# Gate products with the activations as stationary operand, woven between expert products

## The chip, the cores and the metric

The kernel runs on one core of one Trainium2 chip. The metric is the device time of one execution in microseconds. A core has a matrix engine (TensorE, PE in the profile; its loads of stationary operands are shown as PEld), a vector engine (DVE), an activation engine (ACT), GpSimd (POOL) and a queue engine (SP). Each engine takes its own instructions in order and waits for the others through semaphores.

## What is computed

Eight batches of grouped-query attention (16 query heads, 4 key and value heads, 384 positions, head size 64), then a mixture of experts over the 8 x 384 = 3072 tokens of 1024 values. A gate picks one of 4 groups and then one of 4 experts of that group for each token; the token goes through that expert's two layers alone, and its result is scaled by the gate's two probabilities.

```python
attn = softmax(scale * q @ k.T) @ v               # per batch and head
x = attn.transpose(0, 2, 1, 3).reshape(3072, 1024)
g_logits = x @ w_group                            # 1024 x 4
g_idx = argmax(g_logits, axis=1)
e_logits = xg @ w_expert[g]                       # 1024 x 4, for the tokens of group g
e_idx = argmax(e_logits, axis=1)
h = relu(xg[mask_e] @ w1[g, e])                   # 1024 x 1024
out[tok_idx] = g_w * e_w * (h @ w2[g, e])         # 1024 x 1024
```

Both gates together are 20 columns (`NW`): 4 for the groups, 16 for the experts.

## The kernel before

**Stages.** The order of the instructions is written out by hand. For each batch b from 2 on there is an attention stage (`Attn.run`) and then a block (`block(b)`). The block runs the experts' layers for batch b - 1 on PE, while DVE and ACT normalise the attention output of batch b and cast it to bf16. Batches 0 and 1 are arranged apart: batch 0's first expert layer stands inside the attention of batch 1, and `first_block` holds its second layer.

**Attention.** A unit is one head group and one slice of 64 keys: four bf16 products for the scores (L305), the exponential on ACT (L311), then four f32 products with v (L324). There are 24 units in a batch. POOL adds pairs of exponentials (L331), DVE reduces them for the row sums (L338). Each group's output goes from PSUM to `xT[b]` (f32, 128 partitions x 8 x 384: the 1024 values of a token on partitions and 8 slices, tokens along the free axis). `xT[b]` of batch 1 lives in one of the two buffers of the expert weight w1.

**Normalisation.** `collect` sums what was reduced (L397), `sums` brings it to the right partitions with PE (L405), DVE takes the reciprocal (L409) and `normalise` spreads it and multiplies `xT` in place (L416, L425), a pair of slices at a time. `cast` makes bf16 (`xb`) of it on ACT (L432).

**The experts.** `moe_h` (L606) has 16 products of 384 columns per call, and four calls make the first layer; ACT applies the relu (L608). `ffn_y` (L615) makes the second layer for one chunk of 128 tokens: two halves of 8 products with 512 columns. `y_out` scales and stores.

**One expert per batch, by a guess.** The kernel guesses one expert for a whole batch ahead of time, fetches its weights, and runs all tokens of the batch through it, with zero weight for tokens that belong elsewhere. Whatever (batch, expert) pairs are left over are done in a loop at the end. The guess takes the mean of v over the positions: `guess_mean`, 12 products of 128x128 bf16 stationary operands with one column (L457), a copy to `vm`, and `guess_logits`, 4 products with 20 columns (L473). `first_choice` turns logits of batch 0's guess into a choice; for the other batches the guess is a further row of the gate's softmax. `pick_index` turns the choice into an index, and `pick`, `pick_w1` and `pick_w2` fetch weights on POOL's queue.

**The gate.** `gate_logits` holds the gate's weights stationary (32 columns for each of 8 slices, side by side in four column strips of the array) and lets the 384 tokens of `xT` stream past: 8 f32 products (L443). ACT copies the 32 x 4 partial rows to `lgs` (L447). `gate_tokens` then takes `lgs` as stationary operand, in three chunks of 128 tokens, against a 0/1 matrix that adds the four strips: the logits come out with tokens on partitions (L468, 3 f32 products). `gate_softmax` does the choice on DVE, and the closure it returns (`weights[b]`) later does the probabilities. In a block, `gate_logits` stands between the two halves of y of chunk 1, `gate_tokens` and `guess_mean` after that chunk, and `guess_logits` after the first half of chunk 2. Batch 1's gate stands inside the attention of batch 2, after units 3, 19 and 21 (`second_logits`, `second_gate`, `second_pick`).

PSUM is held in two pairs of tiles, named s and o; each new tile takes the other one of its pair, and waits until that one's last reader is done.

Of the kernel before, what the change touches and what calls it, by code (L numbers as in the profile page):

```python
# [18 lines left out]
def kernel(  # L19
# [51 lines left out]
    def ps_tile(which, shape=None, dtype=F32):  # L71
        if which == "x":
            which = f"o{1 - turn['o']}"
        else:
            turn[which] = 1 - turn[which]
            which += str(turn[which])
        return psum.tile(shape or [P, 2, 512], dtype, name="ps_" + which)
# [113 lines left out]
    cw_all = cpool.tile([P, B, SC, NE], F32)  # L191
    oh_all = cpool.tile([P, B, SC + 1, NE], BF16)
    nc.vector.memset(oh_all[:, B - 1, SC, :], 0.0)
    oh_first = cpool.tile([P, NE], BF16)
    oh1_all = cpool.tile([P, B, NE], F32)
    rem_f = cpool.tile([P, B, NE], F32)
# [41 lines left out]
    def evac(eng, out_, in_):  # L238
        if eng is nc.scalar:
            eng.copy(out=out_, in_=in_)  # L240
        else:
            eng.tensor_copy(out=out_, in_=in_)  # L242
# [190 lines left out]

    lgs = {}

    def gate_logits(b, pt):
        lg = pt[:, 0]
        for jj in range(KQ // 4):  # L440
            for t in range(4):
                kq = 4 * jj + t
                nc.tensor.matmul(out=lg[32 * t:32 * t + 32, :S], lhsT=wg[:, kq, :],  # L443
                                 rhs=xT[b][:, kq, :],
                                 start=(jj == 0), stop=(jj == KQ // 4 - 1))
        ls = gpool.tile([P, S], F32, name="lgs")
        nc.scalar.copy(out=ls, in_=lg[:, :S])  # L447
        lgs[b] = ls

    def guess_mean(b, pt, eng=None):  # L450

        pm = pt[:, 1, :Hkv]
        v16 = vraw[b].rearrange("p h x -> p (h x)").bitcast(BF16)
        for g in range(Hkv):
            for i in range(SC):
                e0 = g * NC * D + i * P
                nc.tensor.matmul(out=pm[:, g:g + 1], lhsT=v16[:, 2 * e0 + 1:2 * (e0 + P):2],  # L457
                                 rhs=onesb[:, :1], start=(i == 0), stop=(i == SC - 1))
        vm = gpool.tile([P, Hkv], BF16, name="vm")
        evac(eng or nc.vector, vm, pm)  # L460
        return vm

    def gate_rows(pt):
        return pt[:, 1, 64:64 + (SC + 1) * NW].rearrange("p (c n) -> p c n", n=NW)

    def gate_tokens(b, glp):
        for c in range(SC):
            nc.tensor.matmul(out=glp[:, c, :], lhsT=lgs[b][:, c * P:(c + 1) * P],  # L468
                             rhs=mod32[:, 0, :NW], start=True, stop=True)

    def guess_logits(vm, glp):
        for g in range(Hkv):
            nc.tensor.matmul(out=glp[:, SC, :], lhsT=vm[:, g:g + 1].to_broadcast([P, P]),  # L473
                             rhs=wgd[:, g, :], start=(g == 0), stop=(g == Hkv - 1))

    def gate_softmax(b, glp, guess, eng=None):

# [77 lines left out]
    e_is = {}  # L555

    def pick_index(b):
        oh = oh_first if b == 0 else oh_all[:, b - 1, SC, :]
        key = gpool.tile([P, NE], F32, name="key")
        nc.vector.scalar_tensor_tensor(key, oh, float(NE), eback, op0=ALU.mult, op1=ALU.add)  # L560
        km = gpool.tile([P, 1], F32, name="km")
        nc.vector.tensor_reduce(out=km, in_=key, axis=AX.X, op=ALU.max)
        oh1 = oh1_all[:, b, :]
        nc.vector.tensor_scalar(oh1, key, km, None, op0=ALU.is_ge)
        t1 = gpool.tile([P, NE], F32, name="t1")
        ef = gpool.tile([P, 1], F32, name="ef")
        nc.vector.scalar_tensor_tensor(t1, eidx, 1.0, oh1, op0=ALU.mult, op1=ALU.mult,
                                       accum_out=ef)
        e_i = gpool.tile([P, 1], I32, name="e_i")
        nc.vector.tensor_copy(out=e_i, in_=ef)  # L570
        e_is[b] = e_i
# [27 lines left out]
            j = 2 * c + h  # L599
            yield slice(h * H2, (h + 1) * H2), 2 * (j % SC) + j // SC  # L600

    def ffn_h(x, w1, hT, f0, which):
        h = ps_tile(which)
        for jj in range(2):
            for kq in range(KQ):
                nc.tensor.matmul(out=h[:, jj, :S], lhsT=w1[:, kq, (f0 + jj) * P:(f0 + jj + 1) * P],  # L606
                                 rhs=x[:, kq, :], start=(kq == 0), stop=(kq == KQ - 1))
        nc.scalar.activation(hT[:, f0:f0 + 2, :], h[:, :, :S], ACT.Relu)  # L608

    def ffn_y(w2, hT, c, which, nhs=(0, 1), y=None):  # L610
        if y is None:
            y = ps_tile(which)
        for nh in nhs:
            for f in range(FQ):
                nc.tensor.matmul(out=y[:, nh, :], lhsT=hT[:, f, c * P:(c + 1) * P],  # L615
                                 rhs=w2[:, f, nh * HALF:(nh + 1) * HALF],
                                 start=(f == 0), stop=(f == FQ - 1))
        return y

    hTs = {}  # L620

    def moe_h(b, f0, which):
        if f0 == 0:
            hTs[b] = xpool.tile([P, FQ, S], BF16, name="hT", bufs=1)
        ffn_h(xb[b], w1s[b], hTs[b], f0, which)

    def y_out(b, c, y, split=False):
        ot = opool.tile([P, DM], F32, name="ot")
# [6 lines left out]
        for ps, x in halves(c):  # L635
            nc.sync.dma_start(out=out_rows(out[b * S:(b + 1) * S])[x], in_=ot[ps])

    def moe_y(b, c, which):
        y_out(b, c, ffn_y(w2s[b], hTs[b], c, which))

    def do(f, *a):
        return lambda: f(*a)
# [21 lines left out]

    def first_guess():
        state["pt"] = ps_tile("x")
        state["vm"] = guess_mean(0, state["pt"], nc.scalar)

    def first_pick():
        glp = gate_rows(state["pt"])  # L670
        guess_logits(state["vm"], glp)
        first_choice(glp)
        pick_index(0)

# [46 lines left out]
        11: [do(cast, 0, 2)],  # L721
        13: [do(cast, 0, 3)],
    })
    moe_h(0, 0, "s")
    pt = ps_tile("x")
    gate_logits(0, pt)
    moe_h(0, 2, "s")
    glp = gate_rows(pt)
    gate_tokens(0, glp)
    vm = guess_mean(1, pt, nc.scalar)  # L730
    collect(1, 0, 2)
    sums(1, 0, 2, "s")
    for m in range(2):
        normalise(1, m)
    moe_h(0, 4, "s")
    guess_logits(vm, glp)
    weights[0] = gate_softmax(0, glp, True, nc.scalar)
    pick_index(1)
    moe_h(0, 6, "s")
# [3 lines left out]
    def first_block():  # L743

        prefetch(1)
        collect(1, 2, Hkv)
        weights[0]()
        out_weights(0)
        cast(1, 0)
        cast(1, 1)  # L750
        moe_y(0, 0, "s")
        y = ffn_y(w2s[0], hTs[0], 1, "s", (0,))
        sums(1, 2, Hkv, "o")
        normalise(1, 2)
        normalise(1, 3)
        ffn_y(w2s[0], hTs[0], 1, "s", (1,), y)
        y_out(0, 1, y)
        cast(1, 2)
        cast(1, 3)
        nc.sync.dma_start(out=xb_dram[1], in_=xb[1])  # L760
        y = ffn_y(w2s[0], hTs[0], 2, "o", (0,))
        at[2] = Attn(2)
        at[2].score(0)
        ffn_y(w2s[0], hTs[0], 2, "o", (1,), y)
        at[2].score(1)
        return {1: [do(y_out, 0, 2, y, True)], 3: [second_logits], 19: [second_gate],
                21: [second_pick]}

    def second_logits():
        gate_logits(1, ps_tile("x"))  # L770

    def second_gate():
        state["pt"] = ps_tile("x")
        gate_tokens(1, gate_rows(state["pt"]))
        state["vm"] = guess_mean(2, state["pt"])

    def second_pick():
        glp = gate_rows(state["pt"])
        guess_logits(state["vm"], glp)
        weights[1] = gate_softmax(1, glp, True, nc.scalar)  # L780
        pick_index(2)

    def prefetch(b):
        pick(b)
# [7 lines left out]
    def block(b):  # L792
        last = b == B - 1
        f = b - 1
        prefetch(b)
        moe_h(f, 0, "s")
        collect(b, 0, Hkv)
        weights[f]()
        out_weights(f)
        moe_h(f, 2, "s")  # L800
        sums(b, 0, Hkv, "o")
        for m in range(4):
            normalise(b, m)
        moe_h(f, 4, "s")
        moe_h(f, 6, "s")
        cast(b, 0)
        cast(b, 1)
        moe_y(f, 0, "s")
        cast(b, 2)
        cast(b, 3)  # L810
        nc.sync.dma_start(out=xb_dram[b], in_=xb[b])
        y = ffn_y(w2s[f], hTs[f], 1, "s", (0,))
        gate_logits(b, ps_tile("o"))
        ffn_y(w2s[f], hTs[f], 1, "s", (1,), y)
        y_out(f, 1, y)
        pt = ps_tile("s")
        glp = gate_rows(pt)
        gate_tokens(b, glp)
        vm = None if last else guess_mean(b + 1, pt)
        y = ffn_y(w2s[f], hTs[f], 2, "o", (0,))  # L820
        if not last:
            guess_logits(vm, glp)
            at[b + 1] = Attn(b + 1)
            at[b + 1].score(0)
        weights[b] = gate_softmax(b, glp, not last)
        if not last:
            pick_index(b + 1)
        ffn_y(w2s[f], hTs[f], 2, "o", (1,), y)
        if not last:
            at[b + 1].score(1)  # L830
            return {1: [do(y_out, f, 2, y, True)]}
        y_out(f, 2, y, True)
        weights[b]()
        out_weights(b)
# [120 lines left out]
```

The softmax here doesn't subtract the row's maximum and nothing guards it: scores larger than these inputs give would overflow.

## Time and profile before

| | us |
|---|---|
| median of 3 runs (381.98 to 382.19) | 381.99 |
| profiled execution | 381.92 |
| its span in the profile | 380.1 |
| PE busy | 364.6 |
| DVE busy | 261.9 |
| ACT busy | 232.6 |
| POOL busy | 147.3 |
| L468, 48 records with 20 columns | 6.0 |
| L443, 128 records with 384 columns | 12.0 |
| L447, 8 copies on ACT | 3.8 |

The span runs from the first to the last instruction that the profiler recorded; 1.8 us of the profiled execution lie around it. An f32 product appears as two weight loads and two matmul records. A matmul's recorded length has the array's latency in it, so the pace is read from the distance between starts. The granted clock of TensorE was 0.996 of full speed on average. One block and the attention before it repeat every 44.2 us.

### The profile page before, as it was taken

What the parts mean: (1) busy time and instruction counts of PE and PEld (TensorE: products, weight loads), DVE (VectorE), ACT (ScalarE), POOL (GpSimd) and SP (SyncE); (2) the same over time, 40 slices, a digit from 0 to 9 for tenths busy, and PEclk for the clock granted to TensorE, in tenths of its full rate; (3) what the DMA queues carried; (4) which work ended last, traced back from release to release, by engine and by line L of the source; (5) the groups of instructions that cost most, each with busy time, mean ns of one, the idle gap of its engine ahead of it and who ended that gap; (6) DMA issues with size and microseconds to landing.
All of it is one profiled execution on the core that took longest, in us unless ns stands there. A gap on an engine that the chain in (4) does not pass through costs nothing.

```text
span 380.1 us, 8950 instructions
## 1 busy us (share of the span) xinstructions
PE 364.6 (96%) x3663; PEld 193.9 (51%) x3663; DVE 261.9 (69%) x494; ACT 232.6 (61%) x315; POOL 147.3 (39%) x116
## 2 busy tenths in 40 slices
PE   8999799999989999999999999999999999999992
PEld 3444356444545455545555455554555456554541
DVE  4789978847689279854998279883798449983130
ACT  4779945768824498256953489344982569544321
POOL 5657730716613077212653047330772036600000
PEclk9999999999999999999999999999999999999998
DMA  8975999999999999899999999999998999199734
GB/s 190 247 115 93 238 211 149 241 237 260 207 160 223 252 248 184 173 211 297 213 148 221 228 278 208 148 220 254 244 185 163 182 282 228 30 207 220 236 68 100
DMA packets 71209, 76.02 MB, mean 200 GB/s; under 512 B 35928, under 2 KB 50264, under 8 KB 71168
## 3 DMA queue, kind: packets, MB, share of 16 engines
q0 software_dynamic: 26640, 41.03, 61.8%
q1 hardware_dynamic: 44096, 33.81, 36.1%
q10 hardware_dynamic: 432, 0.61, 0.5%
q8 instruction: 29, 0.48, 0.5%
q14 instruction: 12, 0.10, 0.1%
HBM read 89.21 MB, written 18.87 MB: 284 GB/s over the span
## 4 chain that ended last, share of the span: by engine, by line
PE 78%; DVE 13%; ACT 6%; issue 2%; ACTq 0%; DVEq 0%; POOLq 0%
PE ps_o L324 22%; PE ps_s L606 18%; PE ps_s L615 14%; PE ps_o L615 7%; PE ps_s L305 7%; ACT e L311 4%; DVE red L338 4%; PE ps_o L443 3%; DVE xT L425 2%; DVE rb L416 2%; PE ps_o L268 1%; PE ps_o L606 1%; DVE w L425 1%; PE ps_s L468 1%; PE ps_o L405 1%
## 5 line engine op out<-in xcount | busy, mean ns | idle before, releaser
L331 POOL TENSOR_TENSOR e<-e 128x768 f32<-128x768 f32 x64 | 116.1, 1830 | 138.5 <-ACT e L311 91.5
L311 ACT ACTIVATE e<-ps_s 128x768 f32<-128x768 f32 x192 | 149.1, 819 | 25.2 <-PE ps_s L305 23.5
L324 PE MATMUL ps_o<-e,v_raw 64*64 64x384 f32 x1536 | 153.8, 482 | 1.6 <-DVE xT L425 1.6
L338 DVE TRANSPOSE_TENSOR_REDUCE red<-e 128x24 f32<-128x768 f32 x128 | 114.1, 946 | 10.5 <-POOL e L331 10.5
L606 PE MATMUL ps_s<-xb,w 128*128 128x384 bf16 x480 | 81.0, 326 | 0.0
L324 PEld LDWEIGHTS ps_o<-e,v_raw 64*64 64x64 f32 x1536 | 61.0, 133 | 28.5 <-issue 20.0
L305 PE MATMUL ps_s<-qT,kT 64*64 64x384 bf16 x768 | 67.1, 327 | 3.0 <-ACT e L311 1.7
L608 ACT ACTIVATE hT<-ps_s 128x768 bf16<-128x768 f32 x30 | 24.3, 811 | 70.9 <-PE ps_s L606 70.9
L606 PEld LDWEIGHTS <-w 128*128 128x128 bf16 x512 | 48.8, 98 | 36.3 <-issue 4.8
L615 PEld LDWEIGHTS <-hT 128*128 128x128 bf16 x384 | 36.0, 98 | 45.4 <-issue 5.4
L615 PE MATMUL ps_s<-w,hT 128*128 128x512 bf16 x248 | 56.4, 379 | 0.0
L305 PEld LDWEIGHTS <-kT 64*64 64x64 bf16 x768 | 29.4, 104 | 42.6 <-issue 39.1
L615 PE MATMUL ps_o<-w,hT 128*128 128x512 bf16 x136 | 32.0, 379 | 0.0
L416 DVE STREAM_TRANSPOSE rb<-inv 128x384 f32<-128x384 f32 x60 | 31.1, 557 | 1.0
L425 DVE TENSOR_TENSOR xT<-xT,rb 128x768 f32<-128x768 f32 x26 | 28.2, 1086 | 0.9
L634 ACT ACTIVATE ot<-ps_s,we 128x1024 f32<-128x1024 f32 x14 | 15.6, 1116 | 19.1 <-PE ps_s L615 19.1
L432 ACT CAST xb<-xT 128x768 bf16<-128x768 f32 x28 | 22.1, 832 | 0.0
L371 DVE COPY xT<-ps_o 128x768 f32<-128x768 f32 x22 | 20.2, 919 | 0.0
L242 DVE CAST vm<-ps_s 128x4 bf16<-128x4 f32 x5 | 0.8, 163 | 27.4 <-PE ps_s L457 27.4
L663 POOL COPY after<-qT 128x1 bf16<-128x1 bf16 x7 | 1.3, 189 | 40.5 <-DMA qT<-q_raw 37.5
L631 DVE TENSOR_SCALAR ot<-ps_o,we 128x512 f32<-128x512 f32 x7 | 5.3, 750 | 15.6 <-ACT ot L630 11.3
L409 DVE RECIPROCAL inv<-ps_o 128x96 f32<-128x96 f32 (+2 forms) x10 | 6.0, 603 | 7.0 <-PE ps_o L405 7.0
(129 smaller groups left out, 189.3 us busy)
## 6 DMA issues: line engine op xcount, KB each, us to landing
w<-in_moe_w_dram POOLq DMA_DIRECT2D x16, 2048.0 KB, 21.9
out_dram<-ot SPq DMA_DIRECT2D x42, 256.0 KB, 7.0
xb_scratch<-xb SPq DMA_DIRECT2D x8, 768.0 KB, 9.8
q_raw<-in_q_dram POOLq DMA_DIRECT2D x7, 768.0 KB, 33.6
v_raw<-in_v_dram SPq DMA_DIRECT2D x14, 384.0 KB, 7.3
out_dram<-ot SPq DMA_DIRECT2D x11, 128.0 KB, 2.3
k<-in_k_dram POOLq DMA_DIRECT2D x7, 192.0 KB, 30.3
w<-in_q_dram POOLq DMA_DIRECT2D x3, 192.0 KB, 7.3
```

The source lines that it names most:

```text
L305: nc.tensor.matmul(out=sT[r * H2:(r + 1) * H2, s, :S], lhsT=kT[b][s * D:(s + 1) * D, slot, ks], rhs=qT[b][s * D:(s + 1) * D, kq * SC:(kq + ...
L311: nc.scalar.activation(e.rearrange("p t (s x) -> p s t x", s=2), sT[:, :, :S].rearrange("p s (t x) -> p s t x", t=2), ACT.Exp, scale=scale)
L324: nc.tensor.matmul(out=oT[t * D:(t + 1) * D, r, :S], lhsT=vraw[b][r * H2:(r + 1) * H2, g, c * D:(c + 1) * D], rhs=self.e[u][r * H2:(r + 1) ...
L331: eng.tensor_add(out=self.e[u], in0=self.e[u], in1=self.e[u + 1])
L338: nc.vector.tensor_reduce(out=reds[self.b][:, g, n].rearrange("p t j -> p (t j)"), in_=self.e[u].rearrange("p t (j x) -> p (t j) x", x=32) ...
L371: nc.vector.tensor_copy(out=dst, in_=src)
L416: nc.vector.transpose(out=rb[:, r].rearrange("p (j x) -> p j x", x=32), in_=inv[b][:, 2 * m + r].unsqueeze(2).to_broadcast([P, NB, 32]))
L425: eng.tensor_mul(out=x, in0=x, in1=rb)
L432: nc.scalar.copy(out=xb[b][:, ks, :], in_=xT[b][:, ks, :])
L606: nc.tensor.matmul(out=h[:, jj, :S], lhsT=w1[:, kq, (f0 + jj) * P:(f0 + jj + 1) * P], rhs=x[:, kq, :], start=(kq == 0), stop=(kq == KQ - 1))
L608: nc.scalar.activation(hT[:, f0:f0 + 2, :], h[:, :, :S], ACT.Relu)
L615: nc.tensor.matmul(out=y[:, nh, :], lhsT=hT[:, f, c * P:(c + 1) * P], rhs=w2[:, f, nh * HALF:(nh + 1) * HALF], start=(f == 0), stop=(f == ...
```

## The change

The gate is done in one step, with `xT` as stationary operand: for each chunk of 128 tokens, 8 f32 products of a 128x128 slice of `xT` with 20 columns of the gate's weights, added up in PSUM; 24 products in place of 8 + 3. `gate_logits`, the copy to `lgs` and the 0/1 matrix's product are gone. `gate_tokens`, `guess_mean` and `guess_logits` no longer emit their products but return them as a list, and `weave` emits such a list one by one, spread evenly behind the products of `ffn_h` or `ffn_y`.

In a block, the guess's means go into the fourth `moe_h`, and the gate and the guess logits into y of chunk 1. For batch 0 the means for batch 1 go into the first `moe_h` and the gate and guess logits into the second. The guess for batch 2 moves into `first_block`, as a choice of its own (`first_choice`), and batch 1's gate moves into the first two `moe_h` of block 2, where the normalisation of batch 2 is also put in another order.

```diff
+    def weave(main, side):
+        k = 0
+        for i, f in enumerate(main):
+            f()
+            while k < len(side) and k * len(main) < (i + 1) * len(side):
+                side[k]()
+                k += 1
+
+    def mm(*a, **kw):
+        return lambda: nc.tensor.matmul(*a, **kw)
+
+    def gate_tokens(b, glp):
+        return [mm(out=glp[:, c, :], lhsT=xT[b][:, kq, c * P:(c + 1) * P], rhs=wg[:, kq, :NW],
+                   start=(kq == 0), stop=(kq == KQ - 1))
+                for c in range(SC) for kq in range(KQ)]
...
-    moe_h(0, 0, "s")
     pt = ps_tile("x")
-    gate_logits(0, pt)
-    moe_h(0, 2, "s")
     glp = gate_rows(pt)
-    gate_tokens(0, glp)
-    vm = guess_mean(1, pt, nc.scalar)
+    moe_h(0, 0, "s", guess_mean(1, pt))
+    vm = mean_copy(pt, nc.scalar)
+    moe_h(0, 2, "s", gate_tokens(0, glp) + guess_logits(vm, glp))
     collect(1, 0, 2)
     sums(1, 0, 2, "s")
...
     moe_h(0, 4, "s")
-    guess_logits(vm, glp)
     weights[0] = gate_softmax(0, glp, True, nc.scalar)
     pick_index(1)
...
-        moe_y(0, 0, "s")
-        y = ffn_y(w2s[0], hTs[0], 1, "s", (0,))
+        pt = ps_tile("o")
+        glp = gate_rows(pt)
+        moe_y(0, 0, "s", guess_mean(2, pt))
+        vm = mean_copy(pt, nc.vector)
+        y = ffn_y(w2s[0], hTs[0], 1, "s", (0,), side=guess_logits(vm, glp))
+        first_choice(glp)
         sums(1, 2, Hkv, "o")
...
-        return {1: [do(y_out, 0, 2, y, True)], 3: [second_logits], 19: [second_gate],
-                21: [second_pick]}
+        pick_index(2)
+        return {1: [do(y_out, 0, 2, y, True)]}
...
-        moe_h(f, 0, "s")
+        gates = []
+        if f == 1:
+            glp = gate_rows(ps_tile("o"))
+            gates = gate_tokens(1, glp)
+        moe_h(f, 0, "s", gates[:12])
         collect(b, 0, Hkv)
-        weights[f]()
-        out_weights(f)
-        moe_h(f, 2, "s")
-        sums(b, 0, Hkv, "o")
-        for m in range(4):
-            normalise(b, m)
-        moe_h(f, 4, "s")
-        moe_h(f, 6, "s")
+        if f == 1:
+            sums(b, 0, Hkv, "o")
+            normalise(b, 0)
+            moe_h(f, 2, "s", gates[12:])
+            normalise(b, 1)
+            weights[f] = gate_softmax(f, glp, False)
+            normalise(b, 2)
+            moe_h(f, 4, "s")
+            normalise(b, 3)
+        else:
+            weights[f]()
+            out_weights(f)
+            moe_h(f, 2, "s")
+            sums(b, 0, Hkv, "o")
+            for m in range(4):
+                normalise(b, m)
+            moe_h(f, 4, "s")
+        pt = ps_tile("o")
+        glp = gate_rows(pt)
+        moe_h(f, 6, "s", [] if last else guess_mean(b + 1, pt))
+        if f == 1:
+            weights[f]()
+            out_weights(f)
         cast(b, 0)
         cast(b, 1)
+        guess = [] if last else guess_logits(mean_copy(pt, nc.scalar), glp)
         moe_y(f, 0, "s")
...
-        y = ffn_y(w2s[f], hTs[f], 1, "s", (0,))
-        gate_logits(b, ps_tile("o"))
-        ffn_y(w2s[f], hTs[f], 1, "s", (1,), y)
+        y = ffn_y(w2s[f], hTs[f], 1, "s", side=gate_tokens(b, glp) + guess)
         y_out(f, 1, y)
-        pt = ps_tile("s")
-        glp = gate_rows(pt)
-        gate_tokens(b, glp)
-        vm = None if last else guess_mean(b + 1, pt)
         y = ffn_y(w2s[f], hTs[f], 2, "o", (0,))
         if not last:
-            guess_logits(vm, glp)
             at[b + 1] = Attn(b + 1)
             at[b + 1].score(0)
```

More of the change, by code (lines that the diff above doesn't have):

```diff
@@ L193 @@
     nc.vector.memset(oh_all[:, B - 1, SC, :], 0.0)
+    nc.vector.memset(oh_all[:, 1, SC, :], 0.0)
     oh_first = cpool.tile([P, NE], BF16)
@@ L432, in cast, with guess_mean @@
         nc.scalar.copy(out=xb[b][:, ks, :], in_=xT[b][:, ks, :])
[L436 to L450, printed above, removed]
+    def weave(main, side):
[11 more added lines that the diff above has]
+                for c in range(SC) for kq in range(KQ)]
+    def guess_mean(b, pt):
         pm = pt[:, 1, :Hkv]
         v16 = vraw[b].rearrange("p h x -> p (h x)").bitcast(BF16)
+        side = []
         for g in range(Hkv):
@@ L456, in guess_mean, with mean_copy @@
                 e0 = g * NC * D + i * P
-                nc.tensor.matmul(out=pm[:, g:g + 1], lhsT=v16[:, 2 * e0 + 1:2 * (e0 + P):2],
-                                 rhs=onesb[:, :1], start=(i == 0), stop=(i == SC - 1))
+                side.append(mm(out=pm[:, g:g + 1], lhsT=v16[:, 2 * e0 + 1:2 * (e0 + P):2],
+                               rhs=onesb[:, :1], start=(i == 0), stop=(i == SC - 1)))
+        return side
+    def mean_copy(pt, eng):
         vm = gpool.tile([P, Hkv], BF16, name="vm")
-        evac(eng or nc.vector, vm, pm)
+        evac(eng, vm, pt[:, 1, :Hkv])
         return vm
@@ L464, in gate_rows @@
         return pt[:, 1, 64:64 + (SC + 1) * NW].rearrange("p (c n) -> p c n", n=NW)
[L466 to L469, printed above, removed]
     def guess_logits(vm, glp):
-        for g in range(Hkv):
-            nc.tensor.matmul(out=glp[:, SC, :], lhsT=vm[:, g:g + 1].to_broadcast([P, P]),
-                             rhs=wgd[:, g, :], start=(g == 0), stop=(g == Hkv - 1))
+        return [mm(out=glp[:, SC, :], lhsT=vm[:, g:g + 1].to_broadcast([P, P]), rhs=wgd[:, g, :],
+                   start=(g == 0), stop=(g == Hkv - 1)) for g in range(Hkv)]
     def gate_softmax(b, glp, guess, eng=None):
@@ L557, in pick_index @@
     def pick_index(b):
-        oh = oh_first if b == 0 else oh_all[:, b - 1, SC, :]
+        oh = oh_first if b in (0, 2) else oh_all[:, b - 1, SC, :]
         key = gpool.tile([P, NE], F32, name="key")
@@ L600, in halves, with ffn_h, ffn_y, moe_h @@
             yield slice(h * H2, (h + 1) * H2), 2 * (j % SC) + j // SC
-    def ffn_h(x, w1, hT, f0, which):
+    def ffn_h(x, w1, hT, f0, which, side=()):
         h = ps_tile(which)
[L604 to L607, printed above, removed]
+        weave([mm(out=h[:, jj, :S], lhsT=w1[:, kq, (f0 + jj) * P:(f0 + jj + 1) * P],
+                  rhs=x[:, kq, :], start=(kq == 0), stop=(kq == KQ - 1))
+               for jj in range(2) for kq in range(KQ)], side)
         nc.scalar.activation(hT[:, f0:f0 + 2, :], h[:, :, :S], ACT.Relu)
-    def ffn_y(w2, hT, c, which, nhs=(0, 1), y=None):
+    def ffn_y(w2, hT, c, which, nhs=(0, 1), y=None, side=()):
         if y is None:
             y = ps_tile(which)
[L613 to L617, printed above, removed]
+        weave([mm(out=y[:, nh, :], lhsT=hT[:, f, c * P:(c + 1) * P],
+                  rhs=w2[:, f, nh * HALF:(nh + 1) * HALF], start=(f == 0), stop=(f == FQ - 1))
+               for nh in nhs for f in range(FQ)], side)
         return y
     hTs = {}
-    def moe_h(b, f0, which):
+    def moe_h(b, f0, which, side=()):
         if f0 == 0:
             hTs[b] = xpool.tile([P, FQ, S], BF16, name="hT", bufs=1)
-        ffn_h(xb[b], w1s[b], hTs[b], f0, which)
+        ffn_h(xb[b], w1s[b], hTs[b], f0, which, side)
     def y_out(b, c, y, split=False):
@@ L636, in y_out, with moe_y @@
             nc.sync.dma_start(out=out_rows(out[b * S:(b + 1) * S])[x], in_=ot[ps])
-    def moe_y(b, c, which):
-        y_out(b, c, ffn_y(w2s[b], hTs[b], c, which))
+    def moe_y(b, c, which, side=()):
+        y_out(b, c, ffn_y(w2s[b], hTs[b], c, which, side=side))
     def do(f, *a):
@@ L666, in first_guess @@
         state["pt"] = ps_tile("x")
-        state["vm"] = guess_mean(0, state["pt"], nc.scalar)
+        for f in guess_mean(0, state["pt"]):
+            f()
+        state["vm"] = mean_copy(state["pt"], nc.scalar)
     def first_pick():
         glp = gate_rows(state["pt"])
-        guess_logits(state["vm"], glp)
+        for f in guess_logits(state["vm"], glp):
+            f()
         first_choice(glp)
@@ L765, in first_block @@
         at[2].score(1)
-        return {1: [do(y_out, 0, 2, y, True)], 3: [second_logits], 19: [second_gate],
-                21: [second_pick]}
[L769 to L780, printed above, removed]
         pick_index(2)
+        return {1: [do(y_out, 0, 2, y, True)]}
     def prefetch(b):
```

## The prediction

> **What bounds the kernel now.** I read the page first, engines and then the chain that ended last, then the busy time by stage, then the chain and PE's instructions in order of time inside one steady block. From the page, parts 1 and 4:
>
> ```profile
> PE 364.6 (96%) x3663; PEld 193.9 (51%) x3663; DVE 261.9 (69%) x494; ACT 232.6 (61%) x315; POOL 147.3 (39%) x116
> ...
> PE 78%; DVE 13%; ACT 6%; issue 2%; ACTq 0%; DVEq 0%; POOLq 0%
> ```
>
> PE is the bound, and the chain is PE for 78%. By stage (columns: stretch, its length, then busy us and instructions of PE, weight loads, DVE, ACT, POOL; then clock, DMA share, GB/s):
>
> ```profile
> 86.00:113.50 27.50, 25.39 (x315) 13.85 (x312) 20.34 (x40) 18.13 (x27) 12.50 (x7) 1.00 1.09 207
> ...
> 196.20:222.20 26.00, 25.83 (x190) 13.53 (x190) 16.42 (x41) 11.10 (x15) 4.13 (x7) 1.00 1.01 222
> ```
>
> The block of batch 4 (second line) has PE busy 25.83 of 26.0 us, so nothing absorbs work added there. The attention of batch 2 (first line) has 2.1 us of PE idle. The chain in block 4 (start, length, what):
>
> ```profile
> 207.22 5.18 PE ps_s L615 x24
> 212.40 1.43 PE ps_o L443 x16
> 213.83 1.83 PE ps_s L615 x8
> 215.66 0.58 PE ps_s L468 x6
> 216.24 0.28 PE ps_s L457 x12
> 216.53 1.75 PE ps_o L615 x8
> ```
>
> Gate and guess products stand bare on the path. Their prices come from the timeline of the weight loads and of PE there (start, length, engine):
>
> ```profile
> 215.29 0.85 PEld L468 LDWEIGHTS ps_s<-mod,lgs 128*128 128x128 f32 x6
> 215.98 0.46 PEld L457 LDWEIGHTS <-v_raw 128*128 128x128 bf16 x12
> ```
>
> ```profile
> 212.03 0.38 PE L615 MATMUL ps_s<-w,hT 128*128 128x512 bf16 x1
> 212.33 1.50 PE L443 MATMUL ps_o<-xT,wg 128*32 128x384 f32 x16
> 213.76 1.90 PE L615 MATMUL ps_s<-w,hT 128*128 128x512 bf16 x8
> 215.50 0.74 PE L468 MATMUL ps_s<-mod,lgs 128*128 128x20 f32 x6
> 216.09 0.44 PE L457 MATMUL ps_s<-onesb,v_raw 128*128 128x1 bf16 x12
> 216.39 1.89 PE L615 MATMUL ps_o<-w,hT 128*128 128x512 bf16 x8
> ```
>
> L468 has three f32 products of a 128x128 stationary operand with 20 columns in flight: six records, so an f32 product is two loads and two matmuls. The first load starts at 215.29, with the last expert product, and its matmul starts at 215.50, when that product has streamed (0.214 us): hidden. From 215.50 to 216.09, 0.59 us, there are five exposed f32 loads and the step to a bf16 one. In the single records the f32 loads start 0.111 us apart and the step is 0.029. The twelve bf16 loads of L457 go at 0.025 each (0.30 to 216.39).
>
> **What the Trainium skill says.** "TensorE: Matmul & The Clock Gate", section "LDWEIGHTS (loading the stationary operand)": a load takes its columns divided by 1.2 in ns, 107 for 128 columns; the trace has 111. The same page, "Weight-path perf modes — Fast Weight Load (FWL) and DoubleRow": 128-column loads that are not FP32 are fast; the trace has 25 ns against 111. The same page, "Step-by-step: what each phase is for": the next load is pulled ahead under the running matmul, into a background buffer; the trace shows one load ahead, never two. These three decide the forecast.
>
> **The change part by part.**
>
> *A gate product on its own between expert products.* Its first load hides (0.111 under 0.214, or under the 0.163 of a 384-column product: 16 take 2.65 with start). Then the second f32 load is exposed, 0.111, and then the next expert product's load, which was hidden before, 0.029: 0.140 in all. Two side by side: only the first of four loads hides, 3 x 0.111 + 0.029 = 0.363. No row shows such an alternation, so I bound it. If the expert load too were prefetched, a single costs 0.111. If no load hid, it costs 2 x 0.111 + 0.029 = 0.251. I take 0.140, since both switches of type are in the trace around L468.
>
> *Removed, per batch:* L443 from 212.24 (212.03 + 0.214) to 213.76, 1.52, with the array's change of shape at both ends; L468, 0.59; together 2.11. ACT's copy of lgs (0.48) goes too; ACT is busy 11.1 of 26 us there, so that is worth nothing.
>
> *Added, batches 2 to 6:* 28 side products (24 gate, 4 guess) among 16 main ones: the weave puts them 2, 2, 2, 1 after successive ones. The 24 gates fall as 10 pairs and 4 singles: 3.63 + 0.56 = 4.19. Net +2.08 each, **+10.4 for five**. Batch 7 has no guess: 8 pairs and 8 singles, 4.02, net **+1.91**. Batch 0 has the same 28 in 16: net **+2.08**; PE runs without a gap from 49.9 to 63.3, and DVE's normalisation and ACT wait behind its sums, so it lands on the path.
>
> *Guess products.* Twelve bf16 loads cost 0.30 bare. Woven, the guess's load hides but the expert's is exposed at the same 0.025, so 0.30 again: zero. The four guess logits likewise. The copy of vm moves from DVE to ACT (0.18), behind two casts and 3 us before it is needed: covered; without cover, 0.2 a block.
>
> *Batch 1, moved.* Attention 2 loses three pauses of PE: L443 behind DVE's ot (86.04 to 87.70, 1.66), L468 and L457 behind DVE's copy of xT (101.24 to 103.01, 1.77), L473 (104.65 to 104.94, 0.29): **-3.72**. DVE loses the 3.5 us of softmax and pick from 105.3, so the sums no longer wait at 111.8 (**-1.32**). They now stand one expert step earlier, 4.3 us after attention; DVE's rsum came 3.45 us after it in block 3, so they should find it ready. The gate in block 2: 12 + 12 in 16 + 16, all singles, 24 x 0.140 = **+3.36**. DVE's softmax there ends before guess_mean needs the bank of its logits, by some 2 us.
>
> *What the guess in block 1 makes late.* first_choice stands on DVE before the reciprocal of the sums. Its seven small operations took 1.50 us for batch 0 (27.04 to 28.54). The last guess logit ends near 76.5, so the reciprocal moves from 76.58 to 78.05; behind it stand two normalisations, ACT's last cast (which waited for DVE until 81.21), the first exp, and PE's third score at 82.80. That is **+1.47**, and it covers the 0.4 of guess products in front of it. pick_index(2) comes after them on DVE: covered.
>
> *Queues.* POOL's fetch of w1 for batch 2 now needs the gate's readers of xT[1], which lives in that buffer: done near 113.2, while POOL waits for a transpose until 114.75 anyway. If later, a weight needed at 154 that lands 22 us after its issue still has slack. SP's order is kept.
>
> *Sum:* 10.4 + 1.91 + 2.08 - 3.72 - 1.32 + 3.36 + 1.47 = **+14.2**. Span 380.1 + 14.2 = 394.3. The profiled execution took 381.92, 1.8 around the span, so 396.1; the median of the runs is 0.07 above it: **396**.
>
> **Rivals.**
>
> *Deep prefetch (ends faster).* If several loads could be waiting, the weight port alone would bound a woven stretch. With 512-column products: 48 x 0.111 + 16 x 0.025 = 5.73 against 3.43 of streaming, so gates cost 2.30, +0.19 over before, six times +1.1. Batch 0: 5.73 - 2.60 = 3.13, +1.0. Batch 1 over 32 products: 6.13 - 5.20 = 0.93 in place of 3.36, so its part is -2.64. Sum -0.5; without first_choice's 1.47, which ACT's slack could take, -2.0: **380.0**. It decides from the point where the second f32 load also hides. Against it: L468's loads keep step with its matmuls, one ahead.
>
> *Nothing hides.* 48 x 0.111 + 24 x 0.029 = 6.0 per batch: 7 x 1.8 + 2.7 more, **411**. It needs a drain at each switch of f32 and bf16; against it, the switch at 215.50 cost nothing and the one at 216.09 cost 0.029.
>
> *Absorbed in part.* Attention 2 falls to 19.9 us and the blocks give back a few waits; or pairs cost nearer 0.3: 24 x 6 products at 0.02 to 0.03 less is 3 to 4 us: **391**. Against it: block 4 has 0.17 us idle.
>
> *Within 0.2%.* Only if batch 1's gains were three times what I count. About 0.2% is what a measurement of this kernel can tell from no change.
>
> **How the numbers follow.** Forecast 0.80 (393 to 399), absorbed 0.10 (388 to 393), nothing hides or a new stall 0.06 (399 to 411), deep prefetch 0.03, unchanged 0.01. All but the last two are slower: 0.96. The range 391 to 400.5 leaves out the far part of the absorbed case and of the costly one.
>
> **What would show it.** In each block from batch 2 on: 48 gate records on PE where there were 22, and the 16 expert products of y's token chunk 1, which take 3.43 us bare, stretched to near 7.7. The period of a block goes from 44.2 to 46.3. Attention 2 runs without a gate, with its first exp 1.5 us late, and the sums after it don't wait. f32 loads of the gate under expert products, each second one exposed. Wrong if the woven stretch stays near 5.7, if an alternation costs other than 0.14 for a single and 0.36 for a pair, or if a wait for PSUM, DVE or a weight shows on PE where I saw none.

## The result

The changed kernel takes 400.49 us (median of 4 executions, 397.82 to 403.54) against 382.09 (381.98 to 382.35): a ratio of 1.0483, 95% interval 1.0384 to 1.0582. Its executions fall into two groups, two at 397.8 to 398.0 and two at 403.0 to 403.5; the profiled one, 402.96 with a span of 401.3, is of the second. The runs below show that this difference is the kernel's own. Of 34 executions of the kernel before that were taken with the later runs, one took 476.83 us at a mean clock of 0.754; it is left aside, and nothing here explains it.

From the page of the kernel after, parts 1, 2 (the granted TensorE clock in 40 equal slices, in tenths of full speed) and 4:

```profile
PE 385.7 (96%) x3871; PEld 232.6 (58%) x3871; DVE 262.1 (65%) x498; ACT 229.0 (57%) x311; POOL 147.2 (37%) x116
...
PEclk9999975999999999999999999999999999999998
...
PE 83%; DVE 8%; ACT 6%; issue 2%; ACTq 0%; DVEq 0%
```

PE is busy 21 us more, and its share of the chain goes from 78% to 83%. The clock line shows something that the profile of the kernel before does not have: two slices, from 50 to 70 us, with 0.7 and 0.5.

**A steady block.** Part of the block of batch 4 in order of time, PE and then the weight loads (start, length, engine; L447 is now the line of every product that goes through `mm`, so expert products are told from gate products by their shapes):

```profile
224.23 0.52 PE L447 MATMUL ps_o<-wg,xT 128*128 128x20 f32 x4
224.59 0.38 PE L447 MATMUL ps_s<-w,hT 128*128 128x512 bf16 x1
224.81 0.52 PE L447 MATMUL ps_o<-wg,xT 128*128 128x20 f32 x4
225.17 0.38 PE L447 MATMUL ps_s<-w,hT 128*128 128x512 bf16 x1
225.38 0.52 PE L447 MATMUL ps_o<-wg,xT 128*128 128x20 f32 x4
225.74 0.38 PE L447 MATMUL ps_s<-w,hT 128*128 128x512 bf16 x1
225.96 0.29 PE L447 MATMUL ps_o<-wg,xT 128*128 128x20 f32 x2
226.10 0.38 PE L447 MATMUL ps_s<-w,hT 128*128 128x512 bf16 x1
```

```profile
224.59 0.63 PEld L447 LDWEIGHTS ps_o<-wg,xT 128*128 128x128 f32 x4
225.06 0.18 PEld L447 LDWEIGHTS <-hT 128*128 128x128 bf16 x1
```

A pair stands between 224.81 and 225.17, 0.36 us; a single between 225.96 and 226.10, 0.14. These are the 0.363 and 0.140 of the prediction. The first load of a pair starts at 224.59 with the expert product and hides; the expert product's own load starts at 225.06, only after the pair's last load. A block and its attention repeat every 46.24 us in place of 44.2: +2.05, where +2.08 was predicted. The first expert products of two blocks on the chain (start, length, what):

```profile
209.44 5.31 PE ps_s L447 x32
255.68 5.31 PE ps_s L447 x32
```

**Batch 0's layer.** Busy time from its first expert product to the next score (stretch, length, busy us and instructions of PE, weight loads, DVE, ACT, POOL; then clock, DMA share, GB/s), then the waits of PE there. First the kernel before, then the profiled execution of the kernel after, then another execution of the same kernel, `a_again`, without the fall of the clock:

```profile
49.86:63.30 13.44, 13.44 (x114) 7.94 (x110) 9.87 (x18) 4.16 (x8) 2.22 (x2) 1.00 1.21 194
```

```profile
49.74:72.90 23.16, 22.05 (x140) 16.59 (x137) 10.69 (x21) 3.57 (x7) 2.23 (x2) 0.71 1.00 190
```

```profile
50.02:67.16 17.14, 15.81 (x140) 11.93 (x136) 10.30 (x20) 3.56 (x7) 2.21 (x2) 1.00 1.08 179
```

```profile
PE ps_o L447 <- ACT vm L241: 0.8, 1, 0.8
PE ps_s L447 <- ACT hT L609: 0.5, 1, 0.5
```

The last fence is `a_again`'s waits (engine and line, what it waited for, total, times, longest). From the first expert product's start to the score's, the stretch took 13.45 us before, with no wait of PE in it. It takes 17.14 with two waits that weren't there, and 23.16 when the clock is at half for 13.65 us (55.99 to 69.64). The first wait in `a_again`, the last two expert products ahead of it and the first two gate products behind it:

```profile
52.77 0.48 PE L447 MATMUL ps_s<-xb,w 128*128 128x384 bf16 x2
54.05 0.62 PE L447 MATMUL ps_o<-wg,xT 128*128 128x20 f32 x4 [0.79 <-ACT vm L241]
```

### The profile page after: what moved, and what is told of

Same layout as the page of the kernel before. It is cut to its first block, busy times and chain, and to the rows that moved or that the text cites. A ratio compares the mean times of both kernels' runs of the same rounds, so it can differ in the third digit from the quotient of the medians.

```text
span 401.3 us, 9374 instructions
## 1 busy us (share of the span) xinstructions
PE 385.7 (96%) x3871; PEld 232.6 (58%) x3871; DVE 262.1 (65%) x498; ACT 229.0 (57%) x311; POOL 147.2 (37%) x116
## 4 chain that ended last, share of the span: by engine, by line
PE 83%; DVE 8%; ACT 6%; issue 2%; ACTq 0%; DVEq 0%
PE ps_s L447 34%; PE ps_o L325 22%; PE ps_o L447 17%; PE ps_s L306 7%; ACT e L312 4%; DVE red L339 2%; DVE xT L426 2%; PE ps_o L269 1%; DVE rb L417 1%; PE ps_o L406 1%; ACT ot L629 1%; DVE ps_o L417 1%; DVE w L426 0%; ACT hT L609 0%; PE ps_o L258 0%
## 5 line engine op out<-in xcount | busy, mean ns | idle before, releaser
L312 ACT ACTIVATE e<-ps_s 128x768 f32<-128x768 f32 x192 | 149.0, 819 | 18.7 <-PE ps_s L306 17.1
L447 PE MATMUL ps_s<-xb,w 128*128 128x384 bf16 x480 | 91.9, 334 | 0.3 <-ACT hT L609 0.3
L447 PEld LDWEIGHTS <-w 128*128 128x128 bf16 x512 | 52.0, 107 | 33.6 <-issue 6.5
L447 PE MATMUL ps_s<-w,hT 128*128 128x512 bf16 x248 | 69.1, 378 | 0.0
L447 PEld LDWEIGHTS <-hT 128*128 128x128 bf16 x384 | 42.7, 115 | 31.8 <-issue 1.6
L447 PEld LDWEIGHTS ps_o<-wg,xT 128*128 128x128 f32 x336 | 51.4, 202 | 4.3 <-ACT vm L241 1.2
L447 PE MATMUL ps_o<-wg,xT 128*128 128x20 f32 x336 | 47.3, 250 | 0.8 <-ACT vm L241 0.8
L243 DVE COPY gl<-ps_o 128x80 f32<-128x80 f32 (+1 forms) x7 | 1.6, 235 | 47.3 <-PE ps_o L447 47.3
L447 PE MATMUL ps_o<-w,hT 128*128 128x512 bf16 x136 | 32.0, 379 | 0.0
```

Source lines behind the costliest of these rows:

```text
L312: nc.scalar.activation(e.rearrange("p t (s x) -> p s t x", s=2), sT[:, :, :S].rearrange("p s (t x) -> p s t x", t=2), ACT.Exp, scale=scale)
L447: return lambda: nc.tensor.matmul(*a, **kw)
```

## The experiments

Each edit is shown against the changed kernel, or against the run that its paragraph names; "..." stands for lines left out. The runs of the kernel before that went with them have medians of 382.6 to 383.0.

**1. The same kernel again** (`a_again`).

> The changed kernel once more. The first four executions lay at 397.8, 398.0, 403.0 and 403.5 us, and the profiled one (403.0) shows TensorE's clock at half for 13.65 us inside batch 0's expert layer. Theory (the clock falls in some executions and not in others): two groups again, near 398 and near 403, nothing between; an execution near 398 has no drop of the clock before the tail, and its batch 0 stretch (first expert product to the first score of the next attention part) is about 17.5 us, against 13.5 before and 23.2 with the drop. Rival (the drop is the profiler's or a single chip's chance): all near 398.

Measured: 397.53, 397.91, 402.85 and 403.37. The two groups are there again, and the granted clock, averaged over the span, goes with them: 0.997 and 0.995 against 0.978 twice. The profiled execution (span 395.9) has full clock from its start to the tail. This gives an account free of the clock, below.

**2. Batch 0's gate as it was** (`b_first_two_step`). The lines left out put back the gate's two steps: `gate_logits`, which now also copies the partial rows to `ls`, and `gate_sum`, which returns the three products of the second step.

```diff
...
-    moe_h(0, 0, "s", guess_mean(1, pt))
-    vm = mean_copy(pt, nc.scalar)
-    moe_h(0, 2, "s", gate_tokens(0, glp) + guess_logits(vm, glp))
+    moe_h(0, 0, "s")
+    pt = ps_tile("x")
+    ls = gate_logits(0, pt)
+    moe_h(0, 2, "s")
+    glp = gate_rows(pt)
+    for f in gate_sum(ls, glp) + guess_mean(1, pt):
+        f()
+    vm = mean_copy(pt, nc.scalar)
...
     moe_h(0, 4, "s")
+    for f in guess_logits(vm, glp):
+        f()
```

> Only batch 0's gate is put back as it was (gate_logits, copy, gate_tokens, bare guess); everything else is the changed kernel's. Theory (batch 0 holds 2.1 us of gate work, about 1.1 us of waiting for the copy of the means, about 0.6 of waiting for a relu, and the drop of the clock): no drop in any execution, and 398.0 - 4.0 = 394.0 us, all runs within 0.5. Rival (the clock drop belongs to any woven stretch, also those of later blocks): still two groups.

Measured: 394.01 (393.53 to 394.13), one group, and batch 0's stretch is back at 13.45 us. So batch 0 holds all of the difference between the groups, as far as four executions tell, and 3.7 us besides. The 11 us that remain over the kernel before belong to the later blocks.

**3. The gate ahead of the means** (`c_gate_first`, and again as `c_again`).

```diff
-    moe_h(0, 0, "s", guess_mean(1, pt))
-    vm = mean_copy(pt, nc.scalar)
-    moe_h(0, 2, "s", gate_tokens(0, glp) + guess_logits(vm, glp))
+    moe_h(0, 0, "s", gate_tokens(0, glp))
+    moe_h(0, 2, "s", guess_mean(1, pt))
+    vm = mean_copy(pt, nc.scalar)
...
-    moe_h(0, 4, "s")
+    moe_h(0, 4, "s", guess_logits(vm, glp))
```

> Batch 0's gate stays woven at 28 or 24 in 16, but it comes first (first expert layer call), the means second and the guess logits third, so that no gate product waits for the copy of the means. If the idle gap of about 1 us ahead of the gate is needed for the drop of the clock: one group at 398.0 - 1.1 = 396.9 us. If the thin stretch of weight loads alone is enough: two groups still, near 396.9 and near 402.

> c_gate_first once more with more executions (four so far, 396.3 to 397.5, none with a fall of the clock). If its clock never falls because no gap precedes the thin stretch: all of these near 396.7. If it was chance (four of eight executions of the changed kernel fell): some near 402.

Measured: 396.65 (396.33 to 397.51) and 396.07 (395.45 to 397.08): nine executions, none near 402. No product of the gate waits (a wait of 0.6 us stands behind the gate, ahead of the third layer call), and the stretch takes 15.95 us.

**4. No two gate products side by side** (`d_gate_spread`, and again as `d_again`).

```diff
-    moe_h(0, 2, "s", gate_tokens(0, glp) + guess_logits(vm, glp))
+    gates = gate_tokens(0, glp)
+    moe_h(0, 2, "s", gates[:12])
...
-    moe_h(0, 4, "s")
+    moe_h(0, 4, "s", gates[12:] + guess_logits(vm, glp))
```

> Batch 0's gate is spread over 32 expert products in place of 16, so that no two gate products stand side by side; the wait for the copy of the means stays. By the cost of a single (0.140) against a pair (0.363) it takes 3.36 us in place of 4.19: 398.0 - 0.8 = 397.2 us without a drop of the clock. If the drop comes from how little of the time products stream (0.163 of 0.303 us here, 0.163 of 0.526 in the pairs): no drop, one group. If the wait ahead of it makes the drop: two groups still.

> d_gate_spread once more with more executions: the gap of about 1 us is there, but no gate product stands beside another (products stream for about half the time, against a third in the changed kernel). If the gap alone makes the clock fall in some executions: some near 402. If the thin stretch behind it is needed too: all near 396.8.

Measured: 396.76 (396.25 to 397.61) and 397.04 (396.77 to 397.05): nine executions, none near 402. The stretch takes 16.31 us, 0.83 less than 17.14, as singles against pairs say.

**5. The means in the other bank** (`j_other_bank`). `guess_mean` and its copy use bank 0 of the tile for batch 0, the gate's logits stay in bank 1.

```diff
...
-    moe_h(0, 0, "s", guess_mean(1, pt))
-    vm = mean_copy(pt, nc.scalar)
+    moe_h(0, 0, "s", guess_mean(1, pt, 0))
+    vm = mean_copy(pt, nc.scalar, 0)
```

> The changed kernel with one edit: batch 0's means go to the other PSUM bank of their tile, away from the gate's logits; the order of the products is the same. Theory (the first gate product waits only because ACT still has to copy the means out of the same bank, behind its relu): the wait of about 1.1 us goes, 397.8 - 1.1 = 396.7 us. If that gap is needed for the fall of the clock: one group of runs, none near 403. If the woven stretch falls without it: two groups, 396.7 and near 402. Rival for the wait (any part of the tile is enough to wait for): no change, two groups at 398 and 403.

Measured: 397.74 (396.84 to 403.26, 6 executions), with two at 401.61 and 403.26, at mean clocks of 0.986 and 0.979. My theory of the bank fell: the first gate product still waits 0.8 us for the copy, and the clock still falls in some executions. This program waits for the copy whatever bank of the tile it reads.

**6. The copy after the gate** (`k_copy_later`).

```diff
-    vm = mean_copy(pt, nc.scalar)
-    moe_h(0, 2, "s", gate_tokens(0, glp) + guess_logits(vm, glp))
+    moe_h(0, 2, "s", gate_tokens(0, glp))
+    vm = mean_copy(pt, nc.scalar)
...
-    moe_h(0, 4, "s")
+    moe_h(0, 4, "s", guess_logits(vm, glp))
```

> The changed kernel with batch 0's copy of the means placed after the gate's products in place of before them (the guess logits follow one expert layer call later). Means, gate and expert products keep their order on TensorE. Theory (the copy is what the first gate product waits for, whatever bank it reads): the wait of about 1.1 us goes, and 24 in 16 cost 0.17 less than 28 in 16: 397.8 - 1.3 = 396.5 us. If the gap ahead of the thin stretch is needed for the fall of the clock: no execution near 402. If the thin stretch is enough: some near 402.

Measured: 396.75 (396.17 to 397.01, 5 executions), none near 402. The gate no longer waits, and the stretch takes 15.81 us: it is the order of copy and gate that makes the wait. A wait of 0.4 us behind the gate stays.

**7. The gate bare** (`e_bare`): `b_first_two_step`, with the later blocks' gate behind y of chunk 1 and not woven.

```diff
-        y = ffn_y(w2s[f], hTs[f], 1, "s", side=gate_tokens(b, glp) + guess)
+        y = ffn_y(w2s[f], hTs[f], 1, "s")
+        for g in gate_tokens(b, glp) + guess:
+            g()
```

> b_first_two_step (394.0 us) with one difference: in the blocks of batches 2 to 7 the 24 gate products and 4 guess logits follow bare after y of chunk 1 in place of being woven into it. Theory (one load ahead; a woven single costs 0.140 us, a pair 0.363, a bare gate 47 x 0.111 + 0.029 = 5.25): +1.06 us for each of five batches and +1.23 for the last, 400.5 us, if the clock holds. Rival (weaving hides nothing, a pair or a single costs as much as bare): 394. Whether 5.2 us in which TensorE only loads make its clock fall is open: each such fall would add some us more.

Measured: 417.40 (417.05 to 417.56, 4 executions), with a mean clock of 0.956 in every one. Its granted clock by slices, from the page:

```profile
PEclk9999999999997999969999699998999979998998
```

and, in block 4, the gate's products and the busy time around them, the latter with the same columns as above:

```profile
227.14 6.03 PE L447 MATMUL ps_o<-wg,xT 128*128 128x20 f32 x48
```

```profile
226.80:232.00 5.20, 5.20 (x47) 5.06 (x45) 0.00 (x0) 1.11 (x1) 0.00 (x0) 0.98 1.08 243
232.00:238.90 6.90, 6.67 (x26) 2.95 (x27) 2.90 (x16) 0.81 (x1) 0.00 (x0) 0.52 1.08 300
```

From 227.14 on PE only loads weights and streams 20 columns at a time. At 231.79, before the gate is through, the clock goes to half, for 6.83 us. This happens in each of the six blocks of the profile, 3.4 to 5.3 us after the first gate product: four falls of 6.83 us and two of 3.41, together 34.1 us, which cost at most half of that, 17.1. The gate's form was to cost 6.5; 6.5 + 17.1 is 23.6 at most, and 23.4 was measured over `b_first_two_step`. The rival that weaving hides nothing expected no loss; it is out, since at least 6.3 us remain when the falls are taken off. And weaving has a second use here that I hadn't seen: it keeps the clock up.

**8. The gate in two steps everywhere, the rest of the change kept** (`g_two_step_all`): `gate_logits` between the halves of y of chunk 1 and `gate_sum` after it, and for batch 1 after the first and second `moe_h` of block 2. The guess logits stand bare after the first half of y of chunk 2. Batch 0 is as in `b_first_two_step`.

```diff
...
-        moe_h(f, 0, "s", gates[:12])
+        moe_h(f, 0, "s")
+        if f == 1:
+            ls = gate_logits(1, pt)
...
-            moe_h(f, 2, "s", gates[12:])
+            moe_h(f, 2, "s")
+            for g in gate_sum(ls, glp):
+                g()
...
-        y = ffn_y(w2s[f], hTs[f], 1, "s", side=gate_tokens(b, glp) + guess)
+        y = ffn_y(w2s[f], hTs[f], 1, "s", (0,))
+        ls = gate_logits(b, pt)
+        ffn_y(w2s[f], hTs[f], 1, "s", (1,), y)
         y_out(f, 1, y)
+        for g in gate_sum(ls, glp):
+            g()
         y = ffn_y(w2s[f], hTs[f], 2, "o", (0,))
+        for g in guess:
+            g()
```

> The gate in two steps everywhere (gate_logits, copy, gate_tokens, bare), and all else of the change kept: guess means woven, batch 1's gate in block 2, batch 2's guess in block 1. Theory (the loss is the gate's form, 2.08 us for each of five batches, 1.91 for the last, 1.25 for batch 1): 394.0 - 12.3 - 1.25 = 380.4 us, a little under the kernel before. Rival (the moved work costs more than I count, and the gate's form less): clearly above 382.

Measured: 380.59 (380.30 to 380.85), ratio to the kernel before 0.9947 (0.9930 to 0.9964). The 13.4 us between this and `b_first_two_step` are the gate's form in the blocks from batch 1's on (13.55 predicted), and the rest of the change, without the gate's new form, is a small gain.

**9. The choice later on DVE** (`h_choice_later`), against `g_two_step_all`.

```diff
...
-        first_choice(glp)
+        gl = gpool.tile([P, NW], F32, name="fgl")
+        evac(nc.scalar, gl, glp[:, SC, :])
         sums(1, 2, Hkv, "o")
         normalise(1, 2)
         normalise(1, 3)
+        first_choice(gl)
```

> g_two_step_all, and batch 2's guess logits are copied by ACT so that first_choice can stand on DVE after the two normalisations of batch 1 in place of before the reciprocal. Theory (first_choice makes the chain reciprocal, normalise, cast, exp, score 1.2 us late): 380.4 - 1.1 = 379.3 us, and the wait of PE for the exp at the start of batch 2's attention falls from 1.1 us to some 0.3. Rival (ACT or the score's bank is late anyway): no gain.

Measured: 379.72 (379.46 to 379.94), ratio 0.9923 (0.9907 to 0.9940): 0.9 us for 1.1 expected. PE's wait at the start of batch 2's attention, first in `g_two_step_all`, then in `h_choice_later`:

```profile
PE ps_s L306 <- ACT e L312: 1.1, 1, 1.1
```

```profile
PE ps_s L306 <- ACT e L312: 0.3, 1, 0.3
```

**10. The second step woven** (`i_sum_woven`), and the guess logits with it, against `h_choice_later`.

```diff
-        for g in gate_sum(ls, glp):
-            g()
-        y = ffn_y(w2s[f], hTs[f], 2, "o", (0,))
-        for g in guess:
-            g()
+        y = ffn_y(w2s[f], hTs[f], 2, "o", (0,), side=gate_sum(ls, glp) + guess)
```

> h_choice_later, and in the blocks of batches 2 to 7 the three products of the gate's second step and the guess logits are woven into the first half of y of chunk 2. Theory: three singles at 0.140 in place of 0.59 bare, 6 x 0.17 = 1.0 us less, 378.3 us. Rival (a woven product gains nothing): 379.3.

Measured: 378.60 (378.24 to 379.09), ratio 0.9890 (0.9872 to 0.9908), 1.1 us less than `h_choice_later` where 1.0 was expected; a block and its attention repeat every 44.04 us in place of 44.20. It beats both kernels: weaving pays for products that were there anyway, and does not pay for 24 in place of 11.

## Why the prediction was right and wrong

The account by stages, kernel before against `a_again` (both at full clock up to the tail), from the starts of the products that bound each stage:

| stage | before | after | measured | predicted |
|---|---|---|---|---|
| first layer of batch 0 up to the next score | 13.45 | 17.14 | +3.69 | +2.08 |
| y of batch 0 up to the score behind the late exp | 11.97 | 13.19 | +1.22 | +1.47 |
| from there to the first product of block 2 | 23.59 | 19.98 | -3.61 | -3.72 |
| first layer in block 2 | 12.28 | 14.47 | +2.19 | +2.04 |
| all later, as the rest of the span | | | +12.3 | +12.3 |
| span | 380.1 | 395.9 | +15.8 | +14.2 |

The last row but one is 15.8 less the four above it, so its agreement is that of a remainder; the period of a block tests it directly. Block 2's first layer is 3.36 - 1.32 in the prediction.

**Right.** The cost of a single and of a pair, and with them +2.05 per block. The three rules on weight loads that the prices came from held without a correction. So did the pauses taken out of batch 2's attention, the sums that no longer wait, and DVE's chain made late by `first_choice`; `h_choice_later` shows the last of these by removing it. The guess's products cost no more woven (0.027 us each between two expert products of batch 0) than bare (0.025). Of the rivals, deep prefetch is out (0.36 for a pair, 46.24 us a period), as is "nothing hides" for woven products, and block 4 absorbed nothing.

**Wrong.** The step that failed is "Batch 0 has the same 28 in 16: net +2.08 ... so it lands on the path". It took the price of one gate and put the waits and the clock at nothing. Measured, the +2.08 is +3.69 in `a_again`, and 9.7 us in the profiled execution of the result.

First, two waits. In the kernel before, `moe_h(0, 2)` had nothing from ACT in front of it. The change puts the copy of the means ahead of the gate, and that copy stands on ACT behind a relu of 0.81 us, so the gate's first product waits 0.8 us and then loads with no cover, about 1.1 in all. I had looked at the copy of `vm` only for the later blocks, where it has 3 us of room. Then the next layer call waits 0.5 us for the relu of the one before it, since the 0.9 us of gate and guess products that used to stand between them are gone. 2.08 + 1.1 + 0.5 is 3.7, what was measured. `k_copy_later` and `c_gate_first` take the first of the two away; the second is read from the trace and from the sum alone. The prediction gave 0.06 to its rival of nothing hiding or a new stall: the loads hid as forecast, and the new stall came, from ACT.

Second, the clock. Of 14 executions of the kernels with this order (four of the result's, four of `a_again`, six of `j_other_bank`), 6 took 401.6 to 403.5 us at a mean clock of 0.978 to 0.986. The one of these that has a trace shows TensorE for 13.65 us at half clock in this very stage, worth 5.4 us (401.3 against 395.9); that the other five fell at the same place is read from their times. The runs narrow down what it takes:

| batch 0's stretch | gap ahead | executions with a fall |
|---|---|---|
| pairs, and a single after every third, among 384-column products | about 1 us | 6 of 14 |
| pairs and singles in turn (`c`, `k`) | none | 0 of 14 |
| singles alone (`d`) | about 1 us | 0 of 9 |
| two-step gate (`b`) | none | 0 of 4 |

Between the pairs, expert products stream for 0.163 us of every 0.523, a third of the time; between singles for 0.163 of 0.301, over half. In the later blocks it is 0.215 of 0.575 with pairs, and no profile of a woven gate shows a fall there. In `e_bare` it is nothing, and the clock fell in each of the six blocks. The rows do not separate the gap from the thin stretch, one in which expert products stream for little of the time: `c` and `k` take the gap away, but they also weave 24 products in place of 28, which leaves fewer pairs, and `k` and `d_again` ran on another chip than `a_again` and `j_other_bank`.

The Trainium skill's page "TensorE: Matmul & The Clock Gate", section "What's actually happening", says that the clock is gated by how busy PE has been lately, over free-running windows of 3413 ns. The falls seen here last 3.41, 6.83 and 13.65 us, one, two and four such windows, which agrees.

The kept traces allow one step more. Every stretch between two changes of the clock in them is a whole number of 3.413 us, so the windows can be laid over PE's products. For each window of the expert layers that holds gate products of the new form, no attention product, and starts at full clock, 205 in all, I count the share of the time in which expert products stream (0.163 us each with 384 columns, 0.213 with 512; a few records are missing in the traces, so a share can be a little low):

| window | share | what followed |
|---|---|---|
| the one ahead of the fall in the result's profile (52.57 to 55.99) | 27% | half clock |
| the one ahead of each of the six falls in `e_bare` | 0% | half clock |
| leanest of `j_other_bank`, with the same gap | 30% | full clock |
| leanest of batch 0's stretch in `a_again`, with the same gap | 33% | full clock |
| all others, in the ten profiles with this gate | 31% or more | full clock |

The window of the result's profile holds the whole gap and only 0.25 us of what stands ahead of it; in `j_other_bank` and `a_again` the window starts earlier against the gap and holds more. So one reading fits all profiles: the clock falls when expert products stream in too little of one window, somewhere between 27% and 30% here; a gap matters in so far as it empties a window; and the same kernel falls in some executions and not in others by where the window starts. It was found after the runs, and one fall alone lies near the limit, so it is not shown. Nor is it shown what exactly counts as busy; weight loads don't seem to, since they fill 5.06 of the 5.20 us in the first of `e_bare`'s two stretches above.

The forecast of 396.0 is 1.5 to 2 us under the executions without a fall, and 7 under those with one; the median of 400.49, at the top end of my range, lies between two groups and belongs to neither.

## What to carry to other kernels

Price a small f32 product by its two weight loads, and let only the first of them hide behind a streaming product (0.14 us for one alone, 0.36 for two side by side here): exchanging 11 products, 8 of which stream 384 columns, for 24 that stream 20 columns loses, woven or not, while weaving products that are there anyway gains. Look for stretches in which PE mostly loads, and for idle time ahead of them: they can cost the clock, not only their own length. When two small jobs share a PSUM tile, see which engine's queue the first one's copy stands in before the second is put behind it.

## What the runs showed of the hardware that I had not expected

TensorE's granted clock halves although PE is never idle for long: 3.4 to 5.3 us into a run of f32 loads with 20-column products in every case seen (six of six blocks in the profile, and the same mean clock of 0.956 in all four executions), and, by time and mean clock, in 6 of 14 executions with a gap of about 1 us and a stretch behind it that streams a third of the time. In the profiles, seven of 205 windows of 3.413 us had expert products streaming in 27% or less, and each was followed by half clock; the other 198 had 30% or more, and none was. At half clock a gate pair with its expert product took 0.99 us where it took 0.52 at full clock, so a thin stretch prolongs itself: in batch 0 the fall lasted four windows. In `e_bare`, where dense work follows, it lasted two where 1.0 us or more of the gate was still to come, and one where 0.3 us or less was.
